# A recurrence in steps of eight heads instead of four, and feed-forward products in smaller TensorE tiles

## The chip, the cores and the metric

The kernel runs on one core of a Trainium2 chip. The metric is the device time of one execution in microseconds. The core has five engines that work beside each other: TensorE (PE in the profile; its weight loads are a row of their own, PEld), VectorE (DVE), ScalarE (ACT), GpSimd (POOL) and SyncE (SP, which issues most of the DMAs). Each engine works through its own instructions in order and waits on semaphores for the others.

## The reference

For each of 4 x 8 = 32 heads a 40 x 40 state runs over 768 time steps; the outputs then go through a feed-forward layer with a squared ReLU.

```python
state = zeros((B, H, D, D))                      # B, H, S, D = 4, 8, 768, 40
for t in range(S):
    y[:, :, t] = einsum('bhd,bhde->bhe', rt, state)
    Sa = einsum('bhde,bhe->bhd', state, at)
    state = state * wt[:, :, None, :] - einsum('bhd,bhe->bhde', Sa, bt) \
            + einsum('bhd,bhe->bhde', vt, kt)
...
x = y.transpose(0, 2, 1, 3).reshape(3072, 320)
out = (maximum(x @ w_in, 0) ** 2) @ w_out        # w_in 320 x 2048, w_out 2048 x 320
```

## The kernel before

**Recurrence.** Time is cut into six chunks of 128 steps. For a chunk, `emit_dma` loads the six inputs (NR to NB, 128 time steps x 32 heads x 40), and `emit_prep` prepares them: logarithms and exponentials of cumulated decays on ScalarE (cumulated with f32 matmuls, cs at L157 and L165), scaled copies Kp, Btn, Ap on VectorE (L172 to L175), the chunk's end decay GL2 (rep, L181 to L187), transposes into RT, VT, KT, AT (L198 to L204), and the transposed decay GT (L213, L215). In the transposed tiles two heads share a column block: the even head of a pair (slot 0) lies on partitions 0 to 39, the odd one (slot 1) on 64 to 103.

The heads of a chunk are worked off in eight steps of four heads (`quad_heads`): all four of one slot, so that one step uses one partition half, `pb = 64 * slot`. `stage1` makes two masked 128 x 128 products for each head, Em = mask(K A) through the PSUM tile ee (L245, L248) and CmT = mask(V R) through cc (L251, L254). `stage2` brings in the state S2 and its transpose ST2:

- zp (L267) = state times R, copied to Zb by ScalarE (L271);
- mstp: for each head one matmul with ST2 (L274, 40 rows of weights) and, added to it, one with Em (L276, 128 rows); copied to MstTb (L279);
- xtp: for each head one matmul with Zb (L282, 40 rows) and one with Em and CmT (L284, 128 rows); masked into XmT by VectorE (L287);
- yp: for each head one with Kp (L290) and one with Btn (L292), 40 columns of weights each; VectorE adds Zb (ytmp, L295) and multiplies by GT into YS (L297);
- stp: the new state from Vp, Kp, MstTb and Btn (L304, L306), scaled into S2 (L308), transposed on TensorE (stx, L312) and copied into ST2 (L314).

Each of these PSUM tiles has one buffer: ee, cc, zp, xtp and yp one bank each, mstp, stp and stx together one (`tag="stt"`), and the preparation two (`prep`). All eight banks are used.

In the chunk loop (L320) `stage1` of step q is written before `stage2` of step q - 1, and the preparation of the next chunk is put in after step 4; a compile-time scheduler then sets the order of each engine's instructions, so that preparation is spread among the steps. At the end of a chunk 32 DMAs (L341) put YS into XT0 to XT2, the feed-forward input.

**Feed-forward.** 3,072 tokens are worked off in six blocks of 512. For each of 16 groups of 128 hidden units, three matmuls (L360: 128 columns of weights from WIN, 512 moving columns from XT) add up hp; ScalarE copies it to bf16 (hsb, L366) and VectorE makes relu(h) x h (Gt, L367). Then, for each of four groups of 128 tokens, 16 matmuls (L374: 128 columns of weights from Gt, 320 moving columns of WOUT) add up the output tile op2, which ScalarE copies (osb, L379) and a DMA writes out (L381).

Of the kernel before, what the change touches and what calls it, by code (L numbers as in the profile page):

```python
# [15 lines left out]
def kernel(  # L16
# [12 lines left out]
    nc = tc.nc  # L29
# [203 lines left out]
        prs = [block * 4 + i for i in range(4)]  # L233
        return block, slot, pb, hhs, prs

    class QuadCtx:
        pass

    def stage1(q, chd):
        qc = QuadCtx()  # L240
        RT, VT, KT, AT = chd["RT"], chd["VT"], chd["KT"], chd["AT"]
        block, slot, pb, hhs, prs = quad_heads(q)
        ee = aps.tile([128, 4, L], FP32, name=f"ee{q}", tag="ee", bufs=1)
        for i in range(4):
            nc.tensor.matmul(out=ee[:, i, :], lhsT=KT[pb:pb + D, prs[i], :],  # L245
                             rhs=AT[pb:pb + D, prs[i], :], start=True, stop=True)
        Em = qdp.tile([128, 4, L], BF16, name="Em", tag="Em")
        nc.vector.tensor_tensor(out=Em[:], in0=ee[:], in1=MU4[:], op=ALU.mult)  # L248
        cc = aps.tile([128, 4, L], FP32, name=f"cc{q}", tag="cc", bufs=1)
        for i in range(4):  # L250
            nc.tensor.matmul(out=cc[:, i, :], lhsT=VT[pb:pb + D, prs[i], :],  # L251
                             rhs=RT[pb:pb + D, prs[i], :], start=True, stop=True)
        CmT = qdp.tile([128, 4, L], BF16, name="CmT", tag="CmT")
        nc.vector.tensor_tensor(out=CmT[:], in0=cc[:], in1=MU4[:], op=ALU.mult)  # L254
        qc.Em = Em
        qc.CmT = CmT
        return qc

    def stage2(q, c, chd, qc, YS):
        RT, KT, AT, GT = chd["RT"], chd["KT"], chd["AT"], chd["GT"]  # L260
        Btn, GL2, Kp, Vp = chd["Btn"], chd["GL2"], chd["Kp"], chd["Vp"]
        Em, CmT = qc.Em, qc.CmT
        block, slot, pb, hhs, prs = quad_heads(q)
        pc = block * 4
        zp = aps.tile([128, 4, L], FP32, name=f"zp{q}", tag="zp", bufs=1)
        for i in range(4):
            nc.tensor.matmul(out=zp[pb:pb + D, i, :], lhsT=S2[pb:pb + D, prs[i], :],  # L267
                             rhs=RT[pb:pb + D, prs[i], :],
                             start=(i == 0), stop=(i == 3))
        Zb = qdp.tile([128, 4, L], BF16, name="Zb", tag="Zb", bufs=2)  # L270
        nc.scalar.activation(out=Zb[pb:pb + D, :, :], in_=zp[pb:pb + D, :, :], func=ACTF.Copy)  # L271
        mstp = aps.tile([128, 4, D], FP32, name=f"mstp{q}", tag="stt", bufs=1)
        for i in range(4):
            nc.tensor.matmul(out=mstp[:, i, :], lhsT=AT[pb:pb + D, prs[i], :],  # L274
                             rhs=ST2[pb:pb + D, prs[i], :], start=True, stop=False)
            nc.tensor.matmul(out=mstp[:, i, :], lhsT=Em[:, i, :],  # L276
                             rhs=Vp[:, hhs[i], 0:D], start=False, stop=True)
        MstTb = qdp.tile([128, 4, D], BF16, name="MstTb", tag="MstTb", bufs=2)
        nc.scalar.activation(out=MstTb[:], in_=mstp[:], func=ACTF.Copy, scale=-1.0)  # L279
        xtp = aps.tile([128, 4, L], FP32, name=f"xtp{q}", tag="xtp", bufs=1)  # L280
        for i in range(4):
            nc.tensor.matmul(out=xtp[:, i, :], lhsT=AT[pb:pb + D, prs[i], :],  # L282
                             rhs=Zb[pb:pb + D, i, :], start=True, stop=False)
            nc.tensor.matmul(out=xtp[:, i, :], lhsT=Em[:, i, :],  # L284
                             rhs=CmT[:, i, :], start=False, stop=True)
        XmT = qdp.tile([128, 4, L], BF16, name="XmT", tag="XmT", bufs=2)
        nc.vector.tensor_tensor(out=XmT[:], in0=xtp[:], in1=MUN4[:], op=ALU.mult)  # L287
        yp = aps.tile([128, 4, L], FP32, name=f"yp{q}", tag="yp", bufs=1)
        for i in range(4):
            nc.tensor.matmul(out=yp[pb:pb + D, i, :], lhsT=Kp[:, hhs[i], 0:D],  # L290
                             rhs=CmT[:, i, :], start=(i == 0), stop=False)
            nc.tensor.matmul(out=yp[pb:pb + D, i, :], lhsT=Btn[:, hhs[i], 0:D],  # L292
                             rhs=XmT[:, i, :], start=False, stop=(i == 3))
        ytmp = qdp.tile([128, 4, L], FP32, name="ytmp", tag="ytmp", bufs=2)
        nc.vector.tensor_tensor(out=ytmp[pb:pb + D, :, :], in0=yp[pb:pb + D, :, :],  # L295
                                in1=Zb[pb:pb + D, :, :], op=ALU.add)
        nc.vector.tensor_tensor(  # L297
            out=YS[pb:pb + D, pc:pc + 4, :], in0=ytmp[pb:pb + D, :, :],
            in1=GT[pb:pb + D, pc:pc + 4, 0:L], op=ALU.mult,
        )  # L300
        stp = aps.tile([128, 4, 64], FP32, name=f"stp{q}", tag="stt", bufs=1)
        for i in range(4):
            so = stp[pb:pb + D, i, 0:D]
            nc.tensor.matmul(out=so, lhsT=Vp[:, hhs[i], 0:D], rhs=Kp[:, hhs[i], 0:D],  # L304
                             start=(i == 0), stop=False)
            nc.tensor.matmul(out=so, lhsT=MstTb[:, i, :], rhs=Btn[:, hhs[i], 0:D],  # L306
                             start=False, stop=(i == 3))
        nc.vector.tensor_tensor(out=S2[pb:pb + D, pc:pc + 4, :], in0=stp[pb:pb + D, :, 0:D],  # L308
                                in1=GL2[pb:pb + D, pc:pc + 4, :], op=ALU.mult)
        stx = aps.tile([128, 4, 64], BF16, name=f"stx{q}", tag="stt", bufs=1)  # L310
        for i in range(4):
            nc.tensor.transpose(out=stx[pb:pb + D, i, 0:D], in_=S2[pb:pb + D, prs[i], :],  # L312
                                identity=IDb[pb:pb + D, pb:pb + D])
        nc.scalar.activation(out=ST2[pb:pb + D, pc:pc + 4, :], in_=stx[pb:pb + D, :, 0:D],  # L314
                             func=ACTF.Copy)

    nat_cur = emit_dma(0)
    chd = emit_prep(0, nat_cur)
# [1 line left out]
    for c in range(NCH):  # L320
        if c + 1 < NCH:
            nat_next = emit_dma(c + 1)
        YS = chp.tile([128, NP, L], BF16, name="YS", tag="YS")
        prev_qc = None
        chd_next = None
        for q in range(NQ):
            qc = stage1(q, chd)
            if q > 0:
                stage2(q - 1, c, chd, prev_qc, YS)
            prev_qc = qc  # L330
            if q == NQ // 2 and c + 1 < NCH:
                chd_next = emit_prep(c + 1, nat_next)
        stage2(NQ - 1, c, chd, prev_qc, YS)
        for hh in range(NH):
            pr, slot, pb = head_geom(hh)
            bb = hh // NHH
            h = hh % NHH
            g = h // 3
            row0 = (h % 3) * D
            tok0 = bb * T + c * L  # L340
            nc.sync.dma_start(  # L341
                out=XTg[g][row0:row0 + D, tok0:tok0 + L],
                in_=YS[pb:pb + D, pr, :],
            )
        chd = chd_next
# [9 lines left out]
    for tb in range(NTB):  # L355
        Gt = mwk.tile([128, 16, 512], BF16, name="Gt", tag="Gt")
        for j in range(16):
            hp = mps.tile([128, 512], FP32, name="hp", tag="hp", bufs=3)
            for g in range(3):
                nc.tensor.matmul(  # L360
                    out=hp[:], lhsT=WIN[g][:, j * 128:(j + 1) * 128],
                    rhs=XTg[g][:, tb * 512:(tb + 1) * 512],
                    start=(g == 0), stop=(g == 2),
                )
            hsb = mwk.tile([128, 512], BF16, name="hsb", tag="hsb", bufs=3)
            nc.scalar.activation(out=hsb[:], in_=hp[:], func=ACTF.Copy)  # L366
            nc.vector.scalar_tensor_tensor(  # L367
                out=Gt[:, j, :], in0=hsb[:], scalar=0.0, in1=hsb[:],
                op0=ALU.max, op1=ALU.mult,
            )  # L370
        for s_ in range(4):
            op_ = mps.tile([128, DM], FP32, name="op2", tag="op2", bufs=2)
            for j in range(16):
                nc.tensor.matmul(  # L374
                    out=op_[:], lhsT=Gt[:, j, s_ * 128:(s_ + 1) * 128],
                    rhs=WOUT[:, j, :], start=(j == 0), stop=(j == 15),
                )
            osb = mwk.tile([128, DM], FP32, name="osb", tag="osb")
            nc.scalar.activation(out=osb[:], in_=op_[:], func=ACTF.Copy)  # L379
            tok0 = tb * 512 + s_ * 128  # L380
            nc.sync.dma_start(out=out[tok0:tok0 + 128, :], in_=osb[:])  # L381

# [29 lines left out]
```

## Time and profile before

| | us |
|---|---|
| median of 3 runs | 552.74 |
| lowest and highest run | 548.52, 553.12 |
| span of the profiled execution | 550.1 |
| end of the first loads and the first TensorE steps of the recurrence | about 45 |
| recurrence, to the last YS | about 427 |
| feed-forward matmuls | 432.4 to 546.7 |

Some of the costliest groups of the page, in the order line, engine, operation, tiles, shapes, count, busy us and mean ns of one:

| line | what | count | busy us | mean ns |
|---|---|---|---|---|
| L360 | PE, hp, three groups, 128 x 512 | 282 recorded | 110 | 391 |
| L374 | PE weight loads from Gt | 384 | 37.6 | 98 |
| L367 | DVE, Gt, 128 x 512 | 96 | 62.5 | 692 |
| L366 | ACT, hsb, 128 x 512 | 96 | 57.1 | 597 |
| L297 | DVE, YS, 40 x 512 | 48 | 32.7 | 681 |
| L157 | PE, cs, f32 | 36 | 30.9 | 972 |
| L181 | PE, rep, f32 | 48 | 25.8 | 666 |

A matmul's duration in these rows runs from its start to the modelled end of its last column, and matmuls overlap: 391 ns is the latency of one, while the next one starts 216 ns later. How much a matmul takes of TensorE's time is therefore read from the distance between starts in the timeline, not from the mean of a group. Some matmul records are missing (282 of 288 for L360).

### The profile page before, as it was taken

What the parts mean: (1) busy time and instruction counts of PE and PEld (TensorE: products, weight loads), DVE (VectorE), ACT (ScalarE), POOL (GpSimd) and SP (SyncE); (2) the same over time, 40 slices, a digit from 0 to 9 for tenths busy, and PEclk for the clock granted to TensorE, in tenths of its full rate; (3) what the DMA queues carried; (4) which work ended last, traced back from release to release, by engine and by line L of the source; (5) the groups of instructions that cost most, each with busy time, mean ns of one, the idle gap of its engine ahead of it and who ended that gap; (6) DMA issues with size and microseconds to landing.
All of it is one profiled execution on the core that took longest, in us unless ns stands there. A gap on an engine that the chain in (4) does not pass through costs nothing.

```text
span 550.1 us, 8764 instructions
## 1 busy us (share of the span) xinstructions
PE 500.9 (91%) x3570; PEld 304.5 (55%) x3576; DVE 292.6 (53%) x478; ACT 230.4 (42%) x403; POOL 49.3 (9%) x54
## 2 busy tenths in 40 slices
PE   0609999999999999999999999999999799999997
PEld 0207546655667545765557665576666365566554
DVE  0126448634566446755467553775655536634752
ACT  1705542644125532255324325352112446744762
POOL 9903000011000200002001010000000000000000
PEclk9957566856559558595668755796555799999999
DMA  9999335633327330934108291000000010011011
GB/s 159 189 186 180 53 54 80 76 53 51 53 49 109 54 51 8 146 56 82 27 7 117 39 128 26 6 6 8 7 7 10 4 49 17 33 48 37 19 42 50
DMA packets 163577, 32.69 MB, mean 59 GB/s; under 512 B 158096, under 2 KB 163216, under 8 KB 163536
## 3 DMA queue, kind: packets, MB, share of 16 engines
q1 hardware_dynamic: 161088, 29.50, 34.5%
q0 software_dynamic: 2448, 2.62, 2.8%
q8 instruction: 28, 0.46, 0.4%
q14 instruction: 13, 0.11, 0.1%
HBM read 28.84 MB, written 3.93 MB: 60 GB/s over the span
## 4 chain that ended last, share of the span: by engine, by line
PE 86%; DMA 5%; SPq 3%; ACT 2%; DVE 2%; issue 1%; ACTq 0%; DVEq 0%
PE hp L360 11%; PE trp L198 5%; PE cs L157 5%; PE rep L181 4%; DMA NB<-in_b_dram 4%; SPq L131 3%; PE trw L213 2%; ACT Zb L271 1%; ACT AT L204 1%; DVE Ap L175 1%; PE op_5950 L374 0%; PE op_5910 L374 0%; PE op_5717 L374 0%; PE op_5544 L374 0%; PE op_5371 L374 0%
## 5 line engine op out<-in xcount | busy, mean ns | idle before, releaser
L367 DVE SCALAR_TENSOR_TENSOR Gt<-hsb 128x512 bf16<-128x512 bf16 x96 | 62.5, 692 | 49.6 <-ACT hsb L366 49.6
L366 ACT ACTIVATE hsb<-hp 128x512 bf16<-128x512 f32 x96 | 57.1, 597 | 12.3 <-DMA XT_82<-YS 5.5
L157 PE MATMUL cs<-lnW,UTI 128*128 128x512 f32 (+1 forms) x36 | 30.9, 972 | 18.7 <-ACT lnW L148 18.7
L374 PEld LDWEIGHTS <-Gt 128*128 128x128 bf16 x384 | 37.6, 98 | 15.5
L181 PE MATMUL rep<-GAM,SEL_74 128*128 128x320 f32 x48 | 25.8, 666 | 14.6 <-DVE GL_166 L187 14.2
L360 PE MATMUL hp<-XT_80,WIN_93 128*128 128x512 bf16 x96 | 37.5, 391 | 0.5 <-issue 0.2
L360 PE MATMUL hp<-XT_78,WIN_90 128*128 128x512 bf16 x90 | 35.0, 389 | 3.0 <-ACT hsb L366 2.4
L360 PE MATMUL hp<-XT_82,WIN_96 128*128 128x512 bf16 x96 | 37.6, 392 | 0.0
L297 DVE TENSOR_TENSOR YS<-ytmp,GT 40x512 bf16<-40x512 f32 x48 | 32.7, 681 | 0.5
L274 PEld LDWEIGHTS <-AT 40*128 40x128 bf16 x192 | 19.0, 99 | 20.1 <-issue 13.1
L292 PEld LDWEIGHTS <-Btn 128*40 128x40 bf16 x192 | 24.0, 130 | 11.0 <-issue 9.2
L284 PEld LDWEIGHTS <-Em 128*128 128x128 bf16 x192 | 19.3, 101 | 19.4 <-issue 2.1
L282 PEld LDWEIGHTS <-AT 40*128 40x128 bf16 x192 | 18.7, 98 | 19.1 <-issue 4.7
L290 PEld LDWEIGHTS <-Kp 128*40 128x40 bf16 x192 | 23.6, 123 | 4.1 <-issue 2.2
L276 PEld LDWEIGHTS <-Em 128*128 128x128 bf16 x192 | 19.5, 101 | 10.1 <-issue 2.8
L145 ACT ACTIVATE Rp<-NR 128x1280 bf16<-128x1280 f32 x6 | 7.6, 1269 | 40.7 <-PE trp L198 30.6
L181 PEld LDWEIGHTS rep<-GAM,SEL_74 128*128 128x128 f32 x48 | 11.5, 273 | 19.6 <-issue 17.0
L172 DVE TENSOR_TENSOR Kp<-NK,GAMI 128x1280 bf16<-128x1280 f32 x6 | 8.9, 1488 | 24.3 <-ACT GAMI L160 24.3
L157 PEld LDWEIGHTS cs<-lnW,UTI 128*128 128x128 f32 x36 | 9.1, 306 | 22.8 <-issue 20.8
L143 POOL MEMSET Rp<- 128x768 bf16 x6 | 4.5, 745 | 179.4 <-PE trp L198 179.4
L304 PEld LDWEIGHTS <-Vp 128*40 128x40 bf16 x192 | 15.1, 110 | 9.4 <-issue 7.3
L267 PEld LDWEIGHTS <-S_84 40*40 40x40 bf16 x192 | 14.9, 115 | 9.4 <-issue 6.0
(1138 smaller groups left out, 1074.1 us busy)
## 6 DMA issues: line engine op xcount, KB each, us to landing
NR<-in_r_dram SPq DMA_DIRECT2D x6, 640.0 KB
NK<-in_k_dram SPq DMA_DIRECT2D x6, 640.0 KB
NV<-in_v_dram SPq DMA_DIRECT2D x6, 640.0 KB
NW<-in_w_dram SPq DMA_DIRECT2D x6, 640.0 KB
NA<-in_a_dram SPq DMA_DIRECT2D x6, 640.0 KB
NB<-in_b_dram SPq DMA_DIRECT2D x6, 640.0 KB
out_dram<-osb SPq DMA_DIRECT2D x24, 160.0 KB
WOUT<-in_moe_w_out_dram POOLq DMA_DIRECT2D x1, 1280.0 KB, 14.5
```

Source lines behind the costliest of these rows:

```text
L157: nc.tensor.matmul(out=cs[:, 0:n], lhsT=UTI[:], rhs=lnW[:, s0:s1], start=True, stop=True)
L181: nc.tensor.matmul(out=rep[:, 0:8 * D], lhsT=SEL127[:], rhs=GAM[:, c0:c0 + 8 * D], start=True, stop=True)
L198: nc.tensor.transpose(out=trp[:, j * L:(j + 1) * L], in_=srcv, identity=IDb[:])
L276: nc.tensor.matmul(out=mstp[:, i, :], lhsT=Em[:, i, :], rhs=Vp[:, hhs[i], 0:D], start=False, stop=True)
L284: nc.tensor.matmul(out=xtp[:, i, :], lhsT=Em[:, i, :], rhs=CmT[:, i, :], start=False, stop=True)
L290: nc.tensor.matmul(out=yp[pb:pb + D, i, :], lhsT=Kp[:, hhs[i], 0:D], rhs=CmT[:, i, :], start=(i == 0), stop=False)
L292: nc.tensor.matmul(out=yp[pb:pb + D, i, :], lhsT=Btn[:, hhs[i], 0:D], rhs=XmT[:, i, :], start=False, stop=(i == 3))
L297: nc.vector.tensor_tensor(out=YS[pb:pb + D, pc:pc + 4, :], in0=ytmp[pb:pb + D, :, :], in1=GT[pb:pb + D, pc:pc + 4, 0:L], op=ALU.mult,)
L360: nc.tensor.matmul(out=hp[:], lhsT=WIN[g][:, j * 128:(j + 1) * 128], rhs=XTg[g][:, tb * 512:(tb + 1) * 512], start=(g == 0), stop=(g == 2),)
L366: nc.scalar.activation(out=hsb[:], in_=hp[:], func=ACTF.Copy)
L367: nc.vector.scalar_tensor_tensor(out=Gt[:, j, :], in0=hsb[:], scalar=0.0, in1=hsb[:], op0=ALU.max, op1=ALU.mult,)
L374: nc.tensor.matmul(out=op_[:], lhsT=Gt[:, j, s_ * 128:(s_ + 1) * 128], rhs=WOUT[:, j, :], start=(j == 0), stop=(j == 15),)
```

## The change

1. `quad_heads` gives way to `oct_heads`: a step has eight heads, four of each slot, listed slot 0, slot 1, slot 0, slot 1 and so on. A chunk has four steps instead of eight. The preparation of the next chunk is put in after step 2 of four.
2. In `stage2` the products that add up in one PSUM tile are no longer written head by head. For mst and xtp all eight matmuls with the state (or Zb) come first, then all eight with Em; likewise Kp, then Btn for yp, and Vp, then Mb for stp.
3. Evacuations on ScalarE and VectorE stay one for each slot, with the shapes of before.
4. PSUM: ee and cc share one tag for each slot (e0, e1), xtp has one for each slot (x0, x1), and zp, the two mst, yp, stp and stx go through one tag with two buffers (sm). Eight banks with the two of prep.
5. Feed-forward, first product: each matmul with 128 columns of weights becomes two with 64 columns, which write partitions 0 to 63 and 64 to 127 of hp.
6. Feed-forward, second product: each matmul becomes four of 64 rows x 64 columns. The two row halves of a weight tile add up in two PSUM tiles (op0, op1, two buffers each); ScalarE copies op0 to osa, VectorE adds op1 into osb.

```diff
+    def oct_heads(o):
+        return [(slot, 64 * slot, i, o * 8 + 2 * i + slot, o * 4 + i)
+                for i in range(4) for slot in range(2)]
...
+        for nm, lt, rt in (("e", KT, AT), ("c", VT, RT)):
+            pp = [aps.tile([128, 4, L], FP32, name=f"{nm}{sl}", tag=f"e{sl}", bufs=1)
+                  for sl in range(2)]
+            for slot, pb, i, hh, pr in oct_heads(o):
+                nc.tensor.matmul(out=pp[slot][:, i, :], lhsT=lt[pb:pb + D, pr, :],
+                                 rhs=rt[pb:pb + D, pr, :], start=True, stop=True)
...
+        zp = aps.tile([128, 4, L], FP32, name=f"zp{o}", tag="sm", bufs=2)
+        for slot, pb, i, hh, pr in heads:
+            nc.tensor.matmul(out=zp[pb:pb + D, i, :], lhsT=S2[pb:pb + D, pr, :],
+                             rhs=RT[pb:pb + D, pr, :],
                              start=(i == 0), stop=(i == 3))
...
+        mst = [aps.tile([128, 4, D], FP32, name=f"mst{sl}", tag="sm", bufs=2)
+               for sl in range(2)]
+        for slot, pb, i, hh, pr in heads:
+            nc.tensor.matmul(out=mst[slot][:, i, :], lhsT=AT[pb:pb + D, pr, :],
+                             rhs=ST2[pb:pb + D, pr, :], start=(i == 0), stop=False,
+                             skip_group_check=True)
+        for slot, pb, i, hh, pr in heads:
+            nc.tensor.matmul(out=mst[slot][:, i, :], lhsT=Em[slot][:, i, :],
+                             rhs=Vp[:, hh, 0:D], start=False, stop=(i == 3),
+                             skip_group_check=True)
...
+        yp = aps.tile([128, 4, L], FP32, name=f"yp{o}", tag="sm", bufs=2)
...
+        stp = aps.tile([128, 4, 64], FP32, name=f"stp{o}", tag="sm", bufs=2)
...
+        stx = aps.tile([128, 4, 64], BF16, name=f"stx{o}", tag="sm", bufs=2)
...
-        for q in range(NQ):
+        for q in range(NQ // 2):
...
-            if q == NQ // 2 and c + 1 < NCH:
+            if q == NQ // 4 and c + 1 < NCH:
...
-                nc.tensor.matmul(
-                    out=hp[:], lhsT=WIN[g][:, j * 128:(j + 1) * 128],
-                    rhs=XTg[g][:, tb * 512:(tb + 1) * 512],
-                    start=(g == 0), stop=(g == 2),
-                )
+                for hf in range(2):
+                    nc.tensor.matmul(
+                        out=hp[64 * hf:64 * hf + 64, :],
+                        lhsT=WIN[g][:, j * 128 + 64 * hf:j * 128 + 64 * hf + 64],
+                        rhs=XTg[g][:, tb * 512:(tb + 1) * 512],
+                        start=(g == 0), stop=(g == 2),
+                    )
...
-            op_ = mps.tile([128, DM], FP32, name="op2", tag="op2", bufs=2)
+            ops = [mps.tile([128, DM], FP32, name=f"op{rh}", tag=f"op{rh}", bufs=2)
+                   for rh in range(2)]
             for j in range(16):
-                nc.tensor.matmul(
-                    out=op_[:], lhsT=Gt[:, j, s_ * 128:(s_ + 1) * 128],
-                    rhs=WOUT[:, j, :], start=(j == 0), stop=(j == 15),
-                )
+                for rh in range(2):
+                    for hf in range(2):
+                        t0 = s_ * 128 + hf * 64
+                        nc.tensor.matmul(
+                            out=ops[rh][64 * hf:64 * hf + 64, :],
+                            lhsT=Gt[64 * rh:64 * rh + 64, j, t0:t0 + 64],
+                            rhs=WOUT[64 * rh:64 * rh + 64, j, :],
+                            start=(j == 0), stop=(j == 15),
+                        )
+            osa = mwk.tile([128, DM], FP32, name="osa", tag="osa")
+            nc.scalar.activation(out=osa[:], in_=ops[0][:], func=ACTF.Copy)
             osb = mwk.tile([128, DM], FP32, name="osb", tag="osb")
-            nc.scalar.activation(out=osb[:], in_=op_[:], func=ACTF.Copy)
+            nc.vector.tensor_tensor(out=osb[:], in0=osa[:], in1=ops[1][:], op=ALU.add)
```

More of the change, by code (lines that the diff above doesn't have):

```diff
@@ L234, in quad_heads @@
         return block, slot, pb, hhs, prs
-    class QuadCtx:
+    class OctCtx:
         pass
-    def stage1(q, chd):
-        qc = QuadCtx()
-        RT, VT, KT, AT = chd["RT"], chd["VT"], chd["KT"], chd["AT"]
[L242 to L257, printed above, removed]
@@ L259, in stage2, with stage1 @@
-    def stage2(q, c, chd, qc, YS):
+    def oct_heads(o):
+        return [(slot, 64 * slot, i, o * 8 + 2 * i + slot, o * 4 + i)
+                for i in range(4) for slot in range(2)]
+    def stage1(o, chd):
+        oc = OctCtx()
+        RT, VT, KT, AT = chd["RT"], chd["VT"], chd["KT"], chd["AT"]
+        res = {}
+        for nm, lt, rt in (("e", KT, AT), ("c", VT, RT)):
[4 more added lines that the diff above has]
+                                 rhs=rt[pb:pb + D, pr, :], start=True, stop=True)
+            for slot in range(2):
+                m_ = qdp.tile([128, 4, L], BF16, name=f"m{nm}{slot}", tag=f"m{nm}{slot}", bufs=2)
+                nc.vector.tensor_tensor(out=m_[:], in0=pp[slot][:], in1=MU4[:], op=ALU.mult)
+                res[nm, slot] = m_
+        oc.Em = [res["e", 0], res["e", 1]]
+        oc.CmT = [res["c", 0], res["c", 1]]
+        return oc
@@ L260, in stage2 @@
+    def stage2(o, c, chd, oc, YS):
         RT, KT, AT, GT = chd["RT"], chd["KT"], chd["AT"], chd["GT"]
         Btn, GL2, Kp, Vp = chd["Btn"], chd["GL2"], chd["Kp"], chd["Vp"]
[L262 to L268, printed above, removed]
+        Em, CmT = oc.Em, oc.CmT
+        heads = oct_heads(o)
+        pc = o * 4
+        zp = aps.tile([128, 4, L], FP32, name=f"zp{o}", tag="sm", bufs=2)
+        for slot, pb, i, hh, pr in heads:
+            nc.tensor.matmul(out=zp[pb:pb + D, i, :], lhsT=S2[pb:pb + D, pr, :],
+                             rhs=RT[pb:pb + D, pr, :],
@@ L269, in stage2 @@
                              start=(i == 0), stop=(i == 3))
         Zb = qdp.tile([128, 4, L], BF16, name="Zb", tag="Zb", bufs=2)
[L271 to L293, printed above, removed]
@@ L294, in stage2 @@
-        ytmp = qdp.tile([128, 4, L], FP32, name="ytmp", tag="ytmp", bufs=2)
[L295 to L299, printed above, removed]
-        )
[L301 to L312, printed above, removed]
+        for slot in range(2):
+            pb = 64 * slot
+            nc.scalar.activation(out=Zb[pb:pb + D, :, :], in_=zp[pb:pb + D, :, :],
+                                 func=ACTF.Copy)
@@ new lines, in stage2 @@
+        Mb = []
+        for slot in range(2):
+            m_ = qdp.tile([128, 4, D], BF16, name=f"Mb{slot}", tag=f"Mb{slot}", bufs=2)
+            nc.scalar.activation(out=m_[:], in_=mst[slot][:], func=ACTF.Copy, scale=-1.0)
+            Mb.append(m_)
+        xtp = [aps.tile([128, 4, L], FP32, name=f"xtp{sl}", tag=f"x{sl}", bufs=1)
+               for sl in range(2)]
+        for slot, pb, i, hh, pr in heads:
+            nc.tensor.matmul(out=xtp[slot][:, i, :], lhsT=AT[pb:pb + D, pr, :],
+                             rhs=Zb[pb:pb + D, i, :], start=(i == 0), stop=False,
+                             skip_group_check=True)
@@ new lines, in stage2 @@
+        for slot, pb, i, hh, pr in heads:
+            nc.tensor.matmul(out=xtp[slot][:, i, :], lhsT=Em[slot][:, i, :],
+                             rhs=CmT[slot][:, i, :], start=False, stop=(i == 3),
+                             skip_group_check=True)
+        XmT = []
+        for slot in range(2):
+            m_ = qdp.tile([128, 4, L], BF16, name=f"Xm{slot}", tag=f"Xm{slot}", bufs=2)
+            nc.vector.tensor_tensor(out=m_[:], in0=xtp[slot][:], in1=MUN4[:], op=ALU.mult)
+            XmT.append(m_)
@@ new lines, in stage2 @@
+        yp = aps.tile([128, 4, L], FP32, name=f"yp{o}", tag="sm", bufs=2)
+        for slot, pb, i, hh, pr in heads:
+            nc.tensor.matmul(out=yp[pb:pb + D, i, :], lhsT=Kp[:, hh, 0:D],
+                             rhs=CmT[slot][:, i, :], start=(i == 0), stop=False,
+                             skip_group_check=True)
+        for slot, pb, i, hh, pr in heads:
+            nc.tensor.matmul(out=yp[pb:pb + D, i, :], lhsT=Btn[:, hh, 0:D],
+                             rhs=XmT[slot][:, i, :], start=False, stop=(i == 3),
+                             skip_group_check=True)
@@ new lines, in stage2 @@
+        ytmp = qdp.tile([128, 4, L], FP32, name="ytmp", tag="ytmp", bufs=2)
+        for slot in range(2):
+            pb = 64 * slot
+            nc.vector.tensor_tensor(out=ytmp[pb:pb + D, :, :], in0=yp[pb:pb + D, :, :],
+                                    in1=Zb[pb:pb + D, :, :], op=ALU.add)
+        for slot in range(2):
+            pb = 64 * slot
+            nc.vector.tensor_tensor(
+                out=YS[pb:pb + D, pc:pc + 4, :], in0=ytmp[pb:pb + D, :, :],
+                in1=GT[pb:pb + D, pc:pc + 4, 0:L], op=ALU.mult)
@@ new lines, in stage2 @@
+        stp = aps.tile([128, 4, 64], FP32, name=f"stp{o}", tag="sm", bufs=2)
+        for slot, pb, i, hh, pr in heads:
+            nc.tensor.matmul(out=stp[pb:pb + D, i, 0:D], lhsT=Vp[:, hh, 0:D],
+                             rhs=Kp[:, hh, 0:D], start=(i == 0), stop=False,
+                             skip_group_check=True)
+        for slot, pb, i, hh, pr in heads:
+            nc.tensor.matmul(out=stp[pb:pb + D, i, 0:D], lhsT=Mb[slot][:, i, :],
+                             rhs=Btn[:, hh, 0:D], start=False, stop=(i == 3),
+                             skip_group_check=True)
@@ L313, in stage2 @@
+        for slot in range(2):
+            pb = 64 * slot
+            nc.vector.tensor_tensor(out=S2[pb:pb + D, pc:pc + 4, :],
+                                    in0=stp[pb:pb + D, :, 0:D],
+                                    in1=GL2[pb:pb + D, pc:pc + 4, :], op=ALU.mult)
+        stx = aps.tile([128, 4, 64], BF16, name=f"stx{o}", tag="sm", bufs=2)
+        for slot, pb, i, hh, pr in heads:
+            nc.tensor.transpose(out=stx[pb:pb + D, i, 0:D], in_=S2[pb:pb + D, pr, :],
                                 identity=IDb[pb:pb + D, pb:pb + D])
-        nc.scalar.activation(out=ST2[pb:pb + D, pc:pc + 4, :], in_=stx[pb:pb + D, :, 0:D],
-                             func=ACTF.Copy)
+        for slot in range(2):
+            pb = 64 * slot
+            nc.scalar.activation(out=ST2[pb:pb + D, pc:pc + 4, :],
+                                 in_=stx[pb:pb + D, :, 0:D], func=ACTF.Copy)
@@ L330 @@
             prev_qc = qc
-            if q == NQ // 2 and c + 1 < NCH:
+            if q == NQ // 4 and c + 1 < NCH:
                 chd_next = emit_prep(c + 1, nat_next)
-        stage2(NQ - 1, c, chd, prev_qc, YS)
+        stage2(NQ // 2 - 1, c, chd, prev_qc, YS)
         for hh in range(NH):
@@ L371 @@
         for s_ in range(4):
-            op_ = mps.tile([128, DM], FP32, name="op2", tag="op2", bufs=2)
+            ops = [mps.tile([128, DM], FP32, name=f"op{rh}", tag=f"op{rh}", bufs=2)
+                   for rh in range(2)]
             for j in range(16):
-                nc.tensor.matmul(
-                    out=op_[:], lhsT=Gt[:, j, s_ * 128:(s_ + 1) * 128],
-                    rhs=WOUT[:, j, :], start=(j == 0), stop=(j == 15),
-                )
+                for rh in range(2):
[9 more added lines that the diff above has]
+            nc.scalar.activation(out=osa[:], in_=ops[0][:], func=ACTF.Copy)
             osb = mwk.tile([128, DM], FP32, name="osb", tag="osb")
-            nc.scalar.activation(out=osb[:], in_=op_[:], func=ACTF.Copy)
+            nc.vector.tensor_tensor(out=osb[:], in0=osa[:], in1=ops[1][:], op=ALU.add)
             tok0 = tb * 512 + s_ * 128
```

## The prediction

> **What bounds the kernel now.** I read the page's head, its clock row and its chain of waits first. Columns of the head: engine, busy us, share of the span, instructions.
>
> ```profile
> span 550.1 us, 8764 instructions
> PE 500.9 (91%) x3570; PEld 304.5 (55%) x3576; DVE 292.6 (53%) x478; ACT 230.4 (42%) x403; POOL 49.3 (9%) x54
> ...
> PEclk9957566856559558595668755796555799999999
> ...
> PE 86%; DMA 5%; SPq 3%; ACT 2%; DVE 2%; issue 1%; ACTq 0%; DVEq 0%
> ```
>
> TensorE carries 86% of the chain that ends last. Its granted clock is 0.5 to 0.7 through the recurrence and 1.0 only in the feed-forward stage. Then busy time by stretch, cut where the chunks begin (columns: stretch; busy us and instructions of each engine; clock; DMA share; GB/s):
>
> ```profile
> 109.00:174.00 65.00, 63.52 (x452) 38.71 (x450) 35.99 (x61) 25.41 (x45) 4.71 (x5) 0.61 0.40 63
> 174.00:239.00 65.00, 63.47 (x485) 39.08 (x484) 37.94 (x63) 26.78 (x47) 4.64 (x5) 0.68 0.41 59
> ...
> 370.00:426.00 56.00, 54.68 (x456) 35.36 (x454) 32.08 (x55) 10.87 (x29) 0.00 (x0) 0.54 0.04 8
> ...
> 436.00:550.00 114.00, 110.39 (x650) 63.90 (x653) 59.46 (x92) 64.82 (x115) 0.00 (x0) 0.99 0.10 35
> ```
>
> A middle chunk is 65 us with TensorE busy for 63.5 and VectorE for 38. The last chunk prepares no successor: 56 us. So I looked at what TensorE does in a step, in order of time (start us, duration us, line, tile, weights x columns):
>
> ```profile
> 105.47 0.23 PE L282 MATMUL xtp_946<-Zb,AT 40*128 40x128 bf16 x1
> 105.63 0.23 PE L284 MATMUL xtp_946<-CmT,Em 128*128 128x128 bf16 x1
> 105.79 0.23 PE L282 MATMUL xtp_946<-Zb,AT 40*128 40x128 bf16 x1
> 105.95 0.23 PE L284 MATMUL xtp_946<-CmT,Em 128*128 128x128 bf16 x1
> ...
> ```
>
> Starts are 0.16 us apart where 40-row weights alternate with 128-row ones. Here is a place without that alternation, two groups of 40-row weights on opposite partition halves:
>
> ```profile
> 56.85 0.23 PE L245 MATMUL ee_391<-AT,KT 40*128 40x128 bf16 x1
> 56.86 0.23 PE L251 MATMUL cc_469<-RT,VT 40*128 40x128 bf16 x1
> 56.91 0.22 PE L245 MATMUL ee_391<-AT,KT 40*128 40x128 bf16 x1
> 56.93 0.22 PE L251 MATMUL cc_469<-RT,VT 40*128 40x128 bf16 x1
> ```
>
> Two matmuls per 0.056 us, the time of one (128 columns): the halves run at once. The same with 40-column weights writing opposite halves (L304/L306 slot 0, L290/L292 slot 1):
>
> ```profile
> 374.21 0.18 PE L304 MATMUL stp_4093<-Kp,Vp 128*40 128x40 bf16 x1
> 374.21 0.23 PE L292 MATMUL yp_4138<-XmT,Btn 128*40 128x128 bf16 x1
> 374.23 0.18 PE L306 MATMUL stp_4093<-Btn,MstTb 128*40 128x40 bf16 x1
> 374.26 0.18 PE L304 MATMUL stp_4093<-Kp,Vp 128*40 128x40 bf16 x1
> ```
>
> L304/L306 keep 0.025 us between starts while L292 runs beside them. Last, the feed-forward part of the chain of waits (start, length, what):
>
> ```profile
> 451.44 10.31 PE hp L360 x47
> 461.75 2.17 PE op_5118 L374 x16
> ```
>
> One 512-token block is 10.3 + 4 x 2.17 = 19.05 us; six make the 114. A matmul costs 0.216 (512 columns) or 0.136 us (320) with no gap.
>
> **Recurrence on TensorE.** I added the distances between matmul starts in the chunk 174 to 239. The 64 mstp matmuls (L274/L276) take 8.7 us, the 64 of xtp 11.7, ee, cc and zp 10.5, yp 6.6, stp 2.8, stx 1.7: 42.0. Preparing the next chunk takes 21.4, waits 1.8. At half clock a 128-column matmul of one shape follows its like after 0.107 us, a 40-column one after 0.033, and a change of shape adds 0.11 (0.218 between L282 and L284). After the change a chunk has four steps. Half clock everywhere, opposite halves paired:
> - mstp: 16 pairs and 32 singles x 0.033 = 1.6, 8 shape changes 0.9: 2.5
> - xtp: 48 x 0.107 + 0.9 = 6.0
> - ee, cc, zp: 48 pairs x 0.107 + 0.5 = 5.6
> - yp 32 pairs: 3.8; stp 32 pairs of 40 columns: 1.5; stx 0.9
>
> Sum 20.3 for 42.0. I keep half clock because TensorE will now pause; preparation at that clock is about 24.6 (its 64 transposes x 0.107, 16 x 0.213, the rest as now). Floor: 45 us a chunk.
>
> **VectorE** does the same operations: per step of eight heads 6 x 0.69 (Em, CmT, XmT), 2 x 0.68 (ytmp), 2 x 0.68 (YS), 2 x 0.33 (S2) = 7.5 us, and 9.8 for preparation (3 x 1.49, 4 x 0.69, 8 x 0.32): 40 a chunk. It was idle for 27 of 65; that cover goes.
>
> **The added wait.** zp, the two mst, yp, stp and stx now rotate through two PSUM buffers, where zp and yp had their own. Serial links of a step, from those rows: zp 0.43 + 0.3 until its last matmul is out, two Zb copies 1.2 + 0.15, mst 0.6 + 0.3, xtp beginning once mst is issued 1.3 + 0.3, two XmT 1.4 + 0.1, second half of yp 0.45 + 0.3, two ytmp and two YS 2.8, two S2 0.7, gaps 0.5: about 10.4 us until the next zp may have its buffer. TensorE is in order: while zp, mst or yp waits for its buffer, the later stage1 and preparation matmuls queued behind it wait too. Em and CmT (2.8) fit the 4.5 us in which VectorE has none of this chain. Four steps: 42 us, with some 20 us of TensorE idle inside, for 24.6 of preparation. If preparation hid fully, a chunk would be 46; if none of it did, 42 + 24.6 = 66, no gain. I take 52: 4.6 that don't fit, and some 1.4 a step for links that stand behind a 1.0 us cs matmul or a 1.49 us VectorE piece (an estimate); it is nearer the lower end because both engines interleave preparation freely in the rows of now.
>
> Both zp and stx now put opposite halves into one bank; every overlapping pair in the trace writes two. So 0 (they overlap) to 0.56 a step (they don't). I take 0. The Trainium skill, TensorEngine Tiling, Gotcha 1, says different row tiles can't use one PSUM bank at the same time; by it the sum would be 24 x 0.56 = 13 us higher. No run here shows which.
>
> **Feed-forward.** hp: two 64-column matmuls for each one, 0 us if they overlap as L304 and L292 do. Second product: four 64x64 matmuls of 320 columns for each one, 0 if all four overlap; two were seen at most. Each needs its weights: four loads and matmuls in 0.136 us is 0.034 a pair, and the rows above hold 0.025 in one half and less across two, so 0. A 40-column load fits in 0.025; by that rate 64 columns take 0.04 at most, hidden in the 0.136 of a tile, or, one after another, 0.154 for four: 7 us in all. The Trainium skill, TensorE: Matmul & The Clock Gate, LDWEIGHTS, has columns / 1.2 ns: an estimate of 0.053 each, 0.213 for four in series, 30 us in all. But for 40 columns it gives 0.033, above the 0.025 seen, so I keep 0. Twelve changes of shape 1.3 us; ACT's extra copy and VectorE's 24 adds (0.33 to 0.69, 160 to 512 columns) lie in VectorE's 8.7 us gaps during the second product, save the last: 0.5. Together +2.
>
> **The sum**, against the profiled 550.1: start and first loads to 45 us stay (DMA and preparation 0). First chunk 64 to 51, four chunks 261 to 208, last 56 to 45 (four steps of 10.4 and lead-in): -77. Issues of YS to XT and of the next loads keep their order on SyncE, 8 per group as now: 0. Feed-forward +2: 475. The median of the runs is 2.6 above the span: 478.
>
> **Rivals.**
> 1. Preparation doesn't hide behind the new chain, or splits the runs of eight (four trw matmuls sat inside an xtp run at 106.34) so that shape changes return: chunks of 60 to 64, 40 to 60 us lost: 518 to 538. For it: VectorE at 77% (40 of 52 us) in a serial chain. Against: TensorE's 20 us of gaps a chunk. 0.17.
> 2. TensorE can't issue the feed-forward's 2,112 matmuls fast enough. The densest 4 us of the trace (370.3 to 374.3) hold 56 matmuls, 0.071 each; by that, 256 per block section cost 18 instead of 8.7 us: +56, 534. Against: those stretches were limited by shape changes, and bursts hold 0.028. 0.12.
> 3. Slower: 64-column tiles that write two halves of one bank don't overlap. hp and the second product both double, 6 x 19 = +114: 592. It decides from 75 us on, that is if two thirds of the work lose their overlap. For it: no overlapping pair in the trace shares a bank. Against: array halves are independent in all three shapes. 0.13.
>
> Forecast 0.55 (455 to 505); 0.03 for less than that. **Range** 452 to 540: rivals 1 and 2 inside, rival 3 and tails (0.2) outside. A measurement here tells about 1% from no change: faster 0.82 (forecast, both rivals but their ends), same 0.04, slower 0.14.
>
> **What will show it.** Alternate halves 0.01 to 0.02 apart in zp, xtp, yp; L282's successors apart by 0.107 or 0.056 and no 0.16 within a run; TensorE busy clearly below 90% in the chunks, VectorE near 75%; chunks of 52; hp 10.3 and op 2.17 us as before. Wrong, if hp takes 20, or if chunks stay at 65 with TensorE waiting for VectorE.

## The result, and the profile after

| | before | changed |
|---|---|---|
| median, us | 552.93 (548.52 to 553.45, 4 runs) | 448.43 (446.82 to 453.02, 4 runs) |
| span of the profiled execution, us | 550.1 | 446.4 |
| ratio | | 0.8145, 95% interval 0.8092 to 0.8198 |

The change saves 104 us; 75 were forecast, and the time lies 4 us below the range. Ratios here leave disturbed executions out, so a ratio needn't be the quotient of two medians.

Head and clock row of the page of the changed kernel:

```profile
span 446.4 us, 11665 instructions
PE 364.4 (82%) x5016; PEld 240.1 (54%) x5016; DVE 304.3 (68%) x502; ACT 227.6 (51%) x403; POOL 49.6 (11%) x54
...
PEclk9985899599669965998599859655669999999999
```

The program has 1,440 more matmuls, and TensorE is busy for 136 us less; VectorE's busy time rises by 12 us. The clock row, 5 to 7 in most of the recurrence before, now is 8 or 9 in more than half of it. Busy time by stretch, for two middle chunks, the last chunk to its last YS and the feed-forward stage (columns as before):

```profile
150.10:195.20 45.10, 39.47 (x491) 25.93 (x488) 38.18 (x65) 26.25 (x48) 4.94 (x6) 0.81 0.55 84
195.20:240.50 45.30, 39.17 (x492) 25.75 (x490) 38.98 (x64) 26.80 (x49) 5.20 (x6) 0.85 0.65 96
282.90:317.60 34.70, 28.52 (x375) 20.26 (x373) 26.26 (x45) 10.15 (x26) 0.00 (x0) 0.50 0.05 10
326.50:442.40 115.90, 115.88 (x2094) 77.17 (x2090) 73.39 (x119) 66.19 (x118) 0.00 (x0) 0.98 0.10 35
```

A middle chunk is 45.2 us where it was 65, at a clock of 0.81 to 0.85 where it was 0.61 to 0.68. Part of a step on TensorE, in order of time:

```profile
197.95 0.40 PE L295 MATMUL xtp<-Zb,AT 40*128 40x128 bf16 x8
198.28 0.62 PE L299 MATMUL xtp<-mc,me 128*128 128x128 bf16 x8
198.83 0.40 PE L309 MATMUL yp<-mc,Kp 128*40 128x128 bf16 x8
199.07 0.26 PE L328 MATMUL stp<-Kp,Vp 128*40 128x40 bf16 x8
...
228.31 0.40 PE L269 MATMUL zp<-RT,S 40*40 40x128 bf16 x8
```

The 16 xtp matmuls of eight heads start between 197.95 and 198.83: 0.055 us each, changes of shape included, where 0.16 lay between two starts. Eight paired ones are over in 0.40, eight full ones (L299) in 0.62. The last row is zp: its eight start 3, 66, 4, 52, 3, 53 and 3 ns apart, so the halves overlap although they write one PSUM bank.

Such a whole group of eight is the exception in xtp. The compile-time scheduler mostly ran four of L295, then four of L299, and the other four of each later: over the run 4 groups of L295 hold eight matmuls and 35 hold four. So the halves overlap in zp, yp, stp and stx, and rarely in mst and xtp. Even so, from the first zp to the last, the shape of the weights changes 420 times between neighbouring matmuls, where it changed 1,109 times before (both counted in the traces).

The feed-forward part of the chain of waits (start, length, what):

```profile
345.88 10.48 PE hp L393 x96
356.36 8.82 PE op L412 x256
```

A block is 19.30 us, 0.25 more than before. Four 64x64 matmuls (at 356.59) start 3, 3 and 4 ns after one another and the next four 0.136 us after the first: all four overlap.

Where the 103.8 us between the two spans lie, by the first zp of a chunk (the first feed-forward block's start is put one block's length ahead of the second's): from chunk 0 to chunk 5 326.7 us became 235.5 (-91.2); from there to the first feed-forward block 58.6 became 43.6 (-15.0); from that block to the end 117.7 became 119.9 (+2.2). Together -104.0, start +0.3.

### The profile page after: what moved, and what is told of

The parts are those of the page before. It is cut to its first block, busy times and chain, and to the rows that moved or that the text cites. A ratio compares the mean times of both kernels' runs of the same rounds, so it can differ in the third digit from the quotient of the medians.

```text
span 446.4 us, 11665 instructions
## 1 busy us (share of the span) xinstructions
PE 364.4 (82%) x5016; PEld 240.1 (54%) x5016; DVE 304.3 (68%) x502; ACT 227.6 (51%) x403; POOL 49.6 (11%) x54
## 5 line engine op out<-in xcount | busy, mean ns | idle before, releaser
L393 PE MATMUL hp<-XT,WIN 128*64 128x512 bf16 x576 | 67.5, 396 | 6.5 <-ACT hsb L400 5.3
L393 PEld LDWEIGHTS <-WIN 128*64 128x64 bf16 x576 | 34.9, 114 | 37.7 <-issue 11.9
L412 PE MATMUL op<-WOUT,Gt 64*64 64x320 bf16 x1536 | 53.3, 296 | 0.0
L412 PEld LDWEIGHTS <-Gt 64*64 64x64 bf16 x1536 | 44.4, 107 | 9.5 <-issue 2.5
L319 DVE TENSOR_TENSOR ytmp<-yp,Zb 40x512 f32<-40x512 f32 x48 | 33.0, 688 | 13.5 <-PE yp L313 6.7
L255 DVE TENSOR_TENSOR mc<-c,MU 128x512 bf16<-128x512 f32 x48 | 32.6, 686 | 12.2 <-PE c L251 11.6
L181 PE MATMUL rep<-GAM,SEL 128*128 128x320 f32 x48 | 24.4, 630 | 19.5 <-DVE GL L187 19.5
L255 DVE TENSOR_TENSOR me<-e,MU 128x512 bf16<-128x512 f32 x48 | 32.0, 689 | 10.9 <-PE e L251 10.1
L305 DVE TENSOR_TENSOR Xm<-xtp,MUN 128x512 bf16<-128x512 f32 x48 | 31.3, 684 | 3.5 <-PE xtp L299 2.9
L275 ACT ACTIVATE Zb<-zp 40x512 bf16<-40x512 f32 x48 | 28.3, 590 | 9.8 <-PE zp L269 8.4
```

Of the source, the lines that this page charges most:

```text
L181: nc.tensor.matmul(out=rep[:, 0:8 * D], lhsT=SEL127[:], rhs=GAM[:, c0:c0 + 8 * D], start=True, stop=True)
L255: nc.vector.tensor_tensor(out=m_[:], in0=pp[slot][:], in1=MU4[:], op=ALU.mult)
L305: nc.vector.tensor_tensor(out=m_[:], in0=xtp[slot][:], in1=MUN4[:], op=ALU.mult)
L393: nc.tensor.matmul(out=hp[64 * hf:64 * hf + 64, :], lhsT=WIN[g][:, j * 128 + 64 * hf:j * 128 + 64 * hf + 64], rhs=XTg[g][:, tb * 512:(tb + ...
L412: nc.tensor.matmul(out=ops[rh][64 * hf:64 * hf + 64, :], lhsT=Gt[64 * rh:64 * rh + 64, j, t0:t0 + 64], rhs=WOUT[64 * rh:64 * rh + 64, j, : ...
```

## The experiments

The theory after the result: the gain is TensorE's, most of it from no longer changing the shape of the weights at every matmul; the chunk came out shorter than forecast because the serial chain of a step is shorter and the granted clock higher than I took them. The rivals: that the overlap of the halves, the feed-forward tiles or VectorE account for it.

**Shape changes back, eight heads kept.**

```diff
-        for slot, pb, i, hh, pr in heads:
             nc.tensor.matmul(out=mst[slot][:, i, :], lhsT=Em[slot][:, i, :],
...
-        for slot, pb, i, hh, pr in heads:
             nc.tensor.matmul(out=xtp[slot][:, i, :], lhsT=Em[slot][:, i, :],
```

> Eight heads, halves in turn, but mst and xtp written head by head again (state term, then triangular term). Theory (the gain is mostly that TensorE no longer changes shape): a step has 32 such matmuls and now about 32 changes instead of 4, 28 x 0.11 = 3.1 us, all of it in the serial links of the step: 24 steps x 3.1 = 74, so about 520. Rival (the gain is the overlap of the two halves, and TensorE's gaps of some 15% swallow the changes): below 460.

Measured 528.6 us, ratio to the kernel before 0.958 (0.953 to 0.963): 80 us more than the changed kernel. In this kernel the order of the two loops alone is worth that; its trace has 980 changes of shape, 560 more than the changed kernel. A middle chunk of this kernel, from zp to zp 58 us:

```profile
179.00:237.00 58.00, 54.70 (x488) 32.82 (x484) 37.68 (x64) 26.50 (x48) 4.63 (x6) 0.71 0.41 64
```

TensorE is busy for 94% of it again, where it was 87% in the changed kernel, and the granted clock is back at 0.71.

**Only the order, in the kernel before.**

```diff
+        for i in range(4):
             nc.tensor.matmul(out=mstp[:, i, :], lhsT=Em[:, i, :],
...
+        for i in range(4):
             nc.tensor.matmul(out=xtp[:, i, :], lhsT=Em[:, i, :],
```

(with `start=(i == 0)` and `stop=(i == 3)`, so that the four heads add up in one group.)

> The kernel before, four heads of one half to a step, with only mstp and xtp written state terms first. Theory (shape changes): 12 changes fewer a step, 48 x 12 x 0.11 = 63 us off a TensorE that had no gaps: about 490. Rival (steps of eight heads and the overlap are needed for the gain): 530 or more.

Measured 477.15 us, ratio 0.866 (0.862 to 0.870): 75 us off with two loops split, more than the 63 expected. The trace has 567 changes of shape, 542 fewer than before; at 0.11 us each they make 60 us. The page of this kernel has a mean clock of 0.818 where the kernel before had 0.744, which may be the rest; that wasn't separated.

**Halves not in turn.**

```diff
-                for i in range(4) for slot in range(2)]
+                for slot in range(2) for i in range(4)]
```

> Eight heads, state terms first, but four matmuls of slot 0 and then four of slot 1 instead of taking turns. Theory (shape changes were most of it): 24 pairs of 128 columns and 16 of 40 lose their overlap, 24 x 0.065 + 16 x 0.025 = 2.0 us of TensorE a step at the clock of 0.8, about half of it in the serial links: 24 us in all, 470. Rival (the overlap is most of the gain): over 500.

Measured 459.75 us, ratio 0.826 (0.821 to 0.831) against 0.8145: 6 us by the ratios. But the edit left most of the overlap in place, since the compile-time scheduler sets its own order. A zp of this run still has its eight matmuls over in 0.41 us, as in the changed kernel:

```profile
162.47 0.41 PE L269 MATMUL zp<-RT,S 40*40 40x128 bf16 x8
```

Of the 2,304 matmuls of the steps, 567 start within 20 ns of the matmul before them; in the changed kernel 605 do, in the kernel before 48. So this run gives no price for the overlap. The two runs above bound it from both sides. The four-head kernel with only the order changed has next to no overlap (52 such starts) and saves 75 us already; the kernel with the shape changes put back has the overlap (549) and saves 23. With the feed-forward stage set aside (it costs 2 to 4 us, as shown below), overlap and steps of eight heads together bring some 25 to 33 us of the gain. How that divides between the two is open.

**Feed-forward products of before.** The whole stage as it was.

> The changed recurrence with the feed-forward products of before. Theory (64-column and 64x64 tiles overlap fully and bring nothing): blocks of 19.05 instead of 19.30 us and 0.5 less at the end, so 2 us less than the changed kernel, about 446. Rival (the small tiles help, by keeping one array mode or through the weight loads): slower than the changed kernel by 2 us or more, 451 or over.

Measured 444.81 us, ratio 0.8063 (0.8030 to 0.8095), so 1% or 4 us below the changed kernel, with 3.3 between the profiled spans. The intervals just touch; the size agrees with 0.25 us for each of six blocks and a later end, and nothing speaks for a gain by the small tiles.

**The chain alone.** Loads and preparation of chunks 1 to 5 are left out, and their steps reuse the inputs of chunk 0.

```diff
-        if c + 1 < NCH:
-            nat_next = emit_dma(c + 1)
...
-            if q == NQ // 4 and c + 1 < NCH:
-                chd_next = emit_prep(c + 1, nat_next)
...
-        chd = chd_next
```

> The changed kernel with chunks 1 to 5 using chunk 0's prepared inputs again: their loads and preparation are left out. It measures the bare chain of the steps. Theory now (middle steps of the changed kernel start 8.1 to 8.5 us apart, and 12 us of a 45 us chunk are preparation that doesn't hide at the chunk's end): chunks of 33 to 36, so about 55 us less than the changed kernel, 390. Rival (the recorded step: a chain of 10.4 us that hides nearly all preparation): chunks of 42 and more, 430 or over.

Measured 405.15 us in one run, between the two. The chunks are 37.5 us, steps of 9.4. Its busy time by stretch (as above), and VectorE in order of time:

```profile
140.00:180.00 40.00, 35.17 (x417) 24.13 (x417) 29.66 (x50) 9.54 (x24) 0.00 (x0) 0.50 0.05 10
```

```profile
172.28 0.67 DVE L337 TENSOR_TENSOR S<-stp,GL 40x160 bf16<-40x160 f32 x2
173.12 1.41 DVE L319 TENSOR_TENSOR ytmp<-yp,Zb 40x512 f32<-40x512 f32 x2 [0.17 <-PE yp L313]
174.56 1.41 DVE L323 TENSOR_TENSOR YS<-ytmp,GT 40x512 bf16<-40x512 f32 x2
175.99 1.29 DVE L255 TENSOR_TENSOR me<-e,MU 128x512 bf16<-128x512 f32 x2
178.92 0.69 DVE L255 TENSOR_TENSOR mc<-c,MU 128x512 bf16<-128x512 f32 x1 [1.64 <-PE c L251]
180.00 0.69 DVE L255 TENSOR_TENSOR mc<-c,MU 128x512 bf16<-128x512 f32 x1 [0.38 <-PE c L251]
180.60 1.28 DVE L305 TENSOR_TENSOR Xm<-xtp,MUN 128x512 bf16<-128x512 f32 x2
```

Two things differ from the chain that I had added up. S is made before ytmp, and all 23 following zps start before ytmp and YS have ended (here zp at 174.03): the 2.8 us of ytmp and YS, which I had counted, are out of it. And mc, the mask of the next step's c, does stand in it: VectorE waits 1.64 us for c while xtp is ready. The chain of waits of an earlier step of this run, from c to the next zp (start, length, what), shows the same:

```profile
141.88 0.55 PE c L251 x4
142.45 0.69 DVE mc L255
143.15 1.21 DVE Xm L305 x2
144.40 0.60 PE yp L313 x7
145.00 0.33 PE stx L342 x7
...
145.65 0.31 ACT ST L346
146.00 0.63 PE zp L269 x8
```

Without preparation the clock is 0.50 from the second step on. So at half clock the bare chain is 9.4 us a step, and the changed kernel's chunk is 45.2 - 37.5 = 7.7 us longer. The two ran at different clocks, though. With pieces of preparation among them, the first two steps of a chunk of the changed kernel (zp at 240.5, 249.0, 257.1) take 8.5 and 8.1 us, less than any but the last of the bare chunk's (11.6, 9.5, 9.5 and 6.9). That called for the next experiment.

**More work for TensorE.** The same kernel with ten matmuls of 512 columns written into each step, five after zp and five before the second half of yp, into a PSUM tile that nothing reads (a constant times a constant, left out of the output).

```diff
+        fill(5)
         Zb = qdp.tile([128, 4, L], BF16, name="Zb", tag="Zb", bufs=2)
...
+        fill(5)
         for slot, pb, i, hh, pr in heads:
             nc.tensor.matmul(out=yp[pb:pb + D, i, :], lhsT=Btn[:, hh, 0:D],
```

> e5_no_prep (chunks 1 to 5 reuse chunk 0's prepared inputs; steps of 9.4 us at a granted clock of 0.50, 405 us) with ten matmuls of 512 columns added to each step, five after zp and five before the second half of yp; their results are not used. Theory (a busier TensorE is granted the full clock, and the preparation shortened the steps of the changed kernel in that way): the clock in the steps rises to 0.9 or 1.0, and ten matmuls of 0.216 us lie in TensorE's gaps: steps of 8.0 to 9.0 us, 375 to 397 in all, faster for more work. Rival (the clock stays at 0.5, or the added work stands in the chain): 10 x 0.427 = 4.3 us more a step at the most, 430 to 500.

Measured 390.44 us in one run, 15 less. A stretch with added matmuls, and the one around the last chunk:

```profile
140.00:180.00 40.00, 40.00 (x536) 21.95 (x534) 34.30 (x57) 11.95 (x30) 0.00 (x0) 1.00 0.05 11
220.00:260.00 40.00, 32.96 (x412) 22.68 (x408) 30.47 (x52) 10.15 (x26) 0.00 (x0) 0.50 0.05 11
```

The scheduler moved the added matmuls forward: all 240 ran between 55.6 and 214.7 us, some 50 in each of chunks 1 to 3 (12 to 13 a step, 2.7 us), and none in the last chunk. That gives a comparison inside one run. Chunks 1 to 3 were granted a clock of 1.00 and took 33.3 to 33.9 us, 8.3 to 8.5 a step. The last chunk, without added work, is back at 0.50 and at steps of 9.5 us. So the clock was a term of the sum, and in this kernel the fuller TensorE was granted the higher one. The share of busy time on the page doesn't tell which: it is 88% in the bare chain at 0.50 and 87% in a middle chunk of the changed kernel at 0.81 to 0.85.

**VectorE relieved, twice.** First YS on GpSimd (`nc.gpsimd.tensor_tensor`), then ytmp dropped, with the state term added by TensorE:

```diff
+        for slot, pb, i, hh, pr in heads:
+            nc.tensor.matmul(out=yp[pb:pb + D, i, :], lhsT=S2[pb:pb + D, pr, :],
+                             rhs=RT[pb:pb + D, pr, :], start=(i == 0), stop=False,
...
-            nc.vector.tensor_tensor(out=ytmp[pb:pb + D, :, :], in0=yp[pb:pb + D, :, :],
-                                    in1=Zb[pb:pb + D, :, :], op=ALU.add)
```

> The changed kernel with the multiplication into YS on GpSimd instead of VectorE. VectorE has 37.5 of 45 us in a chunk; this takes 4 x 1.4 = 5.5 off. Theory (VectorE's queue is now what the steps wait for): chunks shorter by 3 to 5 us, 425 to 435. Rival (the ring of two PSUM buffers and TensorE set the pace, and YS already stands aside): within 3 us of the changed kernel; slower, if GpSimd takes over 4 us for a multiplication and YS is late for the chunk's end.

> The changed kernel with the state term of the output added by TensorE: eight more matmuls (S2, RT) into yp, so that VectorE makes YS from yp in one operation and ytmp is gone. VectorE loses 1.4 us a step, TensorE gains some 0.4 and one shape change of 0.11. Theory (ytmp is a link of the chain from XmT to the next mst, and VectorE is the fullest engine): 1.0 to 1.4 us less a step, 24 to 33 us, 415 to 425. Rival (TensorE is still the bound): 24 x 0.5 = 12 us more, 460.

Measured 442.9 us (ratio 0.806, 0.800 to 0.813) and 447.52 us (0.8135, 0.807 to 0.820). Each takes some 30 us from VectorE over the run (304 to 275 and 273 busy), and neither theory's gain came: about 1%, with intervals that overlap, and nothing. VectorE is 85% busy in a middle chunk, but relieving it alone doesn't shorten the kernel. That fits the chain above, in which ytmp and YS don't stand.

**The loads' queue.** From here on with the feed-forward stage of before.

```diff
-            nc.sync.dma_start(
+            nc.gpsimd.dma_start(
                 out=XTg[g][row0:row0 + D, tok0:tok0 + L],
```

> The kernel e3_ffback (changed recurrence, feed-forward of before, 444.8 us) with the 32 DMAs of YS into XT issued by GpSimd, so that the loads of the next chunk no longer stand behind them on SyncE. Theory (the preparation is now itself a chain of some 43 us a chunk, held up by late loads: NB of the chunk at 195 was issued at 199.1 behind five waiting XT copies, and Btn came at 211.9): chunks shorter by 3 to 6 us, 415 to 430. Rival (loads are in time, and the steps' own chain with preparation between sets the pace): within 1% of 444.8, or slower if GpSimd's issues take longer than SyncE's.

> e8_xt_pool together with the output's state term added on TensorE (as in e7_yp_direct, which alone changed nothing). Theory (e7's 1.4 us a step were hidden by the preparation's chain; with loads in time they count): 15 to 30 us less than e8_xt_pool. Rival (VectorE's time lies beside the path anyway): the same as e8_xt_pool within 1%.

The first: 448.06 us, ratio 0.8108 (0.8084 to 0.8131), no gain over 444.8. Both together: 423.08 us (418.21 to 427.58). So neither part alone brings anything, and the two together some 29 us by the ratios (0.8108 to 0.7582, from the repetition below). The traces show where: the last step of a middle chunk, 11.4 to 12.3 us in the changed kernel, takes 8.5 in the first of these runs and 8.0 in the second, but in the first one the chunk's first step grew from 7.7 to 10.8. Two paths of about the same length, where shortening one shows the other, would look like this. That the second one is the loads' place on SyncE is my reading of the one late NB; the compile-time order of all engines changes with such an edit, and that wasn't separated.

> The same kernel as e9_xt_pool_direct, measured with an interval: about 423 (418 to 428). If its two parts only count together, it stays 20 us or more below e7_yp_direct (447.5) and e8_xt_pool (448.1).

> e9_xt_pool_direct with ten unused 512-column matmuls in each of the four steps of the last chunk, which has no preparation and ran at a clock of 0.6. Theory (the clock is granted by how busy TensorE is): the last chunk shorter by 3 to 5 us and the feed-forward stage starts at full clock, 418 to 420. Rival (the added 2.2 us a step stand in the chain): 4 x 2.2 = 9 us more, 432.

Repeated: 425.15 us (417.71 to 430.47), ratio 0.7582 (0.7545 to 0.7619). With added matmuls in the last chunk: 424.83 us, ratio 0.7702 (0.7676 to 0.7728), a miss. The clock there rose, from 0.56 to 0.77 in 30 us of the last chunk, yet that chunk, from its first zp to the start of the last YS, went from 29.8 us (in e9_xt_pool_direct) to 33.7. In these shorter steps the added matmuls seem to stand in the chain. The best kernel of the study is the one without them, at about 0.76 of the kernel before.

## Why the prediction was right or wrong

- **What bounds the kernel, and shape changes.** Right. 6.2 and 5.7 us a chunk were forecast for mstp and xtp, 71 in six chunks, some 13 of it by pairing; splitting the two loops alone saved 75, joining them again cost 80.
- **Overlap of the halves.** Right in kind, and also within one bank, but not in the place that counted most: xtp and mst were summed as pairs, and their groups mostly ran four heads at a time. The price of the overlap stays open; with the steps of eight heads it is some 25 to 33 us. The Trainium skill, TensorEngine Tiling, Gotcha 1, by which different row tiles can't use one bank at a time, would have added 13 us. Here zp's pairs, in different partitions of one bank, started 3 or 4 ns apart; the measurement decides, for this form.
- **"I keep half clock because TensorE will now pause."** Wrong: 0.81 to 0.85 was granted in middle chunks. Only the last chunk, without preparation, ran at 0.50. Full clock in place of half was worth some 4 us a chunk in the bare chain, the added matmuls included (37.5 to 33.3 or 33.9).
- **"about 10.4 us until the next zp may have its buffer".** Mis-sized. The links as listed add up to 10.8. Measured were 9.4 at half clock (four steps 37.5, not 42), with ytmp and YS outside the chain, and at most 8.3 to 8.5 at full clock. Em and CmT don't fit beside it as I put it: mc waits for c inside the chain.
- **"I take 52".** This is the step that put the time outside the range: the chain was taken too long, at half clock throughout, and with 10 us of preparation on top. A middle chunk was 45.2, that is 37.5 of chain at half clock and 7.7 more, where I had 42 and 10; at the full clock, which the chunks had in part, the chain is at most 33.9. Chunks 0 to 4 gave 91.2 us, the forecast for them being 66 (13 + 53); that is 25 of the 29 us between the two savings. The 46 that I named for preparation hidden fully was not a bound, since it was worked out at half clock. And it would have given 448 for the kernel (five chunks, 6 us less each), so the range's lower end, 452, lay above a case that I had named myself.
- **Last chunk** 15.0 for 11: the same shorter steps, 9.5 us each. **Feed-forward** +2.2 for +2 in the profile (about 4 by the ratios with the stage put back): right. Two small sums there are off: 10.3 + 4 x 2.17 makes 18.98, while 19.05 is the distance between blocks, and four loads at 0.04 make 0.16, not 0.154; neither changes the forecast.
- **Rival 1** didn't come. **Rival 2**: 256 matmuls in 8.82 us, 0.034 each, so issue was no limit. **Rival 3**: tiles in one bank overlap; hp 10.48 instead of 20.
- **Weight loads.** The Trainium skill, TensorE: Matmul & The Clock Gate, LDWEIGHTS, gives 0.213 us by estimate for four loads of 64 columns in series; four loads and matmuls took 0.136. They overlap or are faster; this run can't say which.
- **VectorE as the next bound.** It was named as what fills up, at 40 of 52 us; with 38 to 39 of 45, relieving it alone gained at most 1%.

## What to carry to other kernels

Write matmuls of the same weight shape together: a change of shape cost 0.10 to 0.11 us here, two split loops were worth 13% of the kernel, and TensorE looked 91% busy all the while. When an edit lets TensorE pause or fill up, take its clock as a result and work the chain out for both clocks. An engine at 85% in a serial chain needn't be the limit: relieving it alone gave at most 1%, and some 6% only together with a second edit. And look up in the trace whether the compiler kept the order that you wrote: twice here it didn't, and an experiment then measured something else than its name says.

## What the runs showed of the hardware

- Added work made a kernel faster: 12 to 13 unused 512-column matmuls a step raised the granted clock from 0.50 to 1.00 and cut the step from 9.4 to 8.3 or 8.5 us; where none ran, the same run was back at 0.50 and 9.5 us. In shorter steps, in another kernel, they cost time (the last chunk 33.7 us for 29.8).
- Busy by the page didn't mean granted: the kernel before, with TensorE busy 63.5 of 65 us, got 0.61 to 0.68, and the same matmuls with about half the changes of shape got more in less time (mean over the run 0.744 to 0.818).
- Tiles of 64x64 were sustained at four at once for 8.8 us, and diagonal halves overlapped in one PSUM bank (zp's pairs started 3 or 4 ns apart).
